# A product over three rows padded to 128 rows in a transform and two-layer mixture kernel on one Trainium2 core

## The chip, the core and the metric

The kernel runs on one NeuronCore of a Trainium2 chip. The metric is the device time of one execution in microseconds. TensorE (PE; its weight loads are listed apart as PEld), VectorE (DVE), ScalarE (ACT), GpSimd (POOL) and SyncE (SP, which issues DMAs) each run their own queue in the order in which the program wrote it.

## The reference

`x` has 8 batches of 3072 tokens of 256 numbers.

```python
X = np.fft.fft(x, axis=1)
X = np.fft.fft(X, axis=2)
x = X.real.reshape(B * S, D)              # 24576 tokens
h = x @ w_in                              # 256 -> 2048
g = np.maximum(h, 0.0) + np.log1p(np.exp(-np.abs(h)))
x = g @ w_out                             # 2048 -> 256
...
logits = xn @ en.T / tau                  # 8 experts, the best one is taken
h = np.maximum(x[mask] @ w1[e], 0.0)
out[mask] = gate_w[mask, None] * (h @ w2[e])
```

## The kernel before

Every product is done in fp16 with operands split in a high and a low part, so a product of two matrices is three: high by high, high by low, low by high.

**Phase 1** holds the transform, the first layer pair and the routing. The transform of a batch has two parts. `fft_a` transforms over a factor of 48 of the token axis (tile `psa`, result `U_s`); its inputs are folded and split in `x_split`, mostly on GpSimd (L487 to L492, L594 to L596). `fft_bc` then makes, for each of 8 tiles of a batch, the transform over the features (`psb`, evacuated to `vh` and `vl`) and the rest of the token axis (`psc`, evacuated to `pqh` and `pql`).

The real part of the transform is symmetric: tokens m and S - m share their cosine part and differ in the sign of the sine part. The kernel therefore keeps an even part P and an odd part Q of a tile (192 columns, 193 in the first tile of a batch), and folds `w_in` likewise. The even part has 129 features (0 to 128) and the odd one 127. A TensorE product contracts at most 128 rows, so feature 128 of the even part stands alone: the product `psd` (L705 to L712) makes its row three times over, by a weight operand that repeats one column three times, and L714 to L718 turn it into the tile `r3` (`pq3`) with the rows (high, high, low). Its partner `w128_s` holds the rows (high, low, high) of the weight row 128, filled by three DMAs (L396). One three-row product then stands for the three split products of that feature.

A **unit** is one tile by a quarter of the 2048 hidden features (four blocks of 128): 8 batches x 8 tiles x 4 quarters = 256 units. For each unit:

- `uv_u`: the even part `pu`, four groups of four products (L745 to L748), the last of each with the three-row operands;
- `uv_v`: the odd part `pv`, four groups of three products (L760 to L762);
- ScalarE copies `pu` to `h` (L772), DVE adds and subtracts `pv` (L779, L780), which gives the two mirrored halves of the tokens;
- softplus: ScalarE's Abs, Exp and Ln (L788, L793, L797), then DVE (L802);
- the split of the result: `gh` on GpSimd (L813 to L817), `gl` on DVE (L826);
- `unit_g2`: the products with `w_out` into three accumulators `G`, and at a tile's end the copies to `rows` (L863) and the router.

The order is written out by hand. Each iteration of the main loop names the steps in a string (`ORDER`): `pu` and `pv` of the present unit, the softplus of the one before, `gl` of the one before that, `G` of the one three back, and between them up to three steps of a transform (`f1`, `f2`, `f3`), the scale of the next batch and the router. The transform of batch b + 1 runs beside the units of batch b, `fft_a` in about the first half of them, `fft_bc` in the second. `pu` and `pv` have one PSUM tile each, and the transform has one bank (`F`) for all its products.

```python
mm(o, win_s[:, 0, 0, fs], hh[:, 0, 0:n], True, False)
mm(o, win_s[:, 0, 0, fs], ll[:, 0, 0:n], False, False)
mm(o, win_s[:, 0, 1, fs], hh[:, 0, 0:n], False, False)
mm(o, w128_s[:, fs], r3[:, 0:n], False, True)
```

All matmuls stand on one line (L205, the helper `mm`), so the profile tells them apart by tile: `pu`, `pv`, `psd`, `G`. In the trace `w128_s` is called `w_s` and `r3` is called `pq`.

**Phase 2** (from about 2430 us) gathers the routed tokens of each expert and runs the expert's two layers (`psH`, `psO`).

Of the kernel before, what the change touches and what calls it, by code (L numbers as in the profile page):

```python
# [79 lines left out]
def _tables():  # L80
    scale = 2.0 ** 13
    qs = [(0, 0), (24, 0)]
    for k1 in range(1, 24):
        qs += [(k1, 0), (k1, 1)]
    fa = np.zeros((96, 2, 48))
    a = np.arange(48)
    for q, (k1, im) in enumerate(qs):
        c, s = _trig(a * k1, 48)
        for bb in range(2):
            fa[2 * a + bb, bb, q] = -s if im else c  # L90
    fa = fa.reshape(96, 96)
    # x[d] + x[256-d], x[d] - x[256-d]; for d = 0 x[0] + x[128], x[0] - x[128]
    c, s = _trig(np.arange(129)[:, None] * np.arange(129)[None], 256)
    db = np.zeros((128, 385))
    db[:, 0:129] = c[0:128]
    db[0, 1:129:2] = 0.0
    db[0, 130:258:2] = 1.0
    db[1:, 258:385] = s[1:128, 1:128]
    pos = np.arange(64)
    bv = 32 * (pos % 2) + pos // 2  # L100
    mc, ms = [], []
    for g, cl in enumerate(_columns()):
        m = np.array(cl)[None]
        c, s = _trig(bv[:, None] * m, S)
        if g == 0:
            z = m % 48 == 0
            mc.append(np.concatenate([c * z, c * ~z]))
            ms.append(np.concatenate([-s * z, -s * ~z]))
        else:
            mc.append(np.concatenate([c, s]))  # L110
            ms.append(np.concatenate([-s, c]))
    mcs = np.stack([np.concatenate(mc, 1), np.concatenate(ms, 1)], 1)
    out = {}
    for n, t in (("fa", fa), ("db", db), ("mcs", mcs)):
        hi = (t * scale).astype(np.float16)
        lo = (t * scale - hi.astype(np.float64)).astype(np.float16)
        out[n] = np.ascontiguousarray(np.stack([hi, lo], 1))
    tid = np.zeros((128, NB * NT * 3), np.int32)
    cols = _columns()
    for b in range(NB):  # L120
        for ti in range(NT):
            cl = sum(cols[3 * ti:3 * ti + 3], [])
            toks = cl + [(S - m) % S for m in cl[2 if ti == 0 else 0:]]
            o = (b * NT + ti) * 3
            tid[:, o:o + 3] = (np.array(toks) + b * S).reshape(3, 128).T
    out["tid"] = tid
    out["ident"] = np.eye(128, dtype=np.float32)
    tri = np.zeros((128, 256), np.float16)
    tri[:, :128] = np.triu(np.ones((128, 128)), 1)
    tri[:, 128:] = 1.0  # L130
    out["tri"] = tri
    misc = np.zeros((128, 128 + 8 + 8 + 8), np.float32)
    misc[:, :128] = np.arange(128)[None]
    misc[:, 128:136] = (E - np.arange(E))[None]
    misc[:, 136:144] = (np.arange(E) * CAP)[None]
    misc[2, 144] = -1.0
    misc[1:, 145] = 1.0
    out["misc"] = misc
    return out
# [3 lines left out]
def fft_moe_moe(ctx, tc, x, w_in, w128, w_out, emb, tau, w1, w2, fa, db, mcs, tid, ident, tri, misc, out,  # L143
# [23 lines left out]
    U_s = bigf.tile([128, 2, 2, 48, 64], F16, name="U_s")       # hi/lo, c, q, pos  # L167
# [7 lines left out]
    win_s = big.tile([128, 2, 2, FF], F16, name="win_s")      # (even, odd) x (hi, lo)  # L175
    w128_s = big.tile([3, FF], F16, name="w128_s")
# [19 lines left out]
    def fps(name):  # L196
        """a bank for the transform and for small products; at the start four of them in turn."""
        if boot[2]:
            boot[1] = (boot[1] + 1) % 4
            if boot[1]:  # L200
                return psG.tile([128, 512], F32, tag=f"G{boot[1] - 1}", name=name)
        return psF.tile([128, 512], F32, tag="F", name=name)
# [4 lines left out]
    # A background chain is a generator: a plain yield lets the others go on; a yield of a pair of  # L207
    # functions asks for a small product (the first) in spare PSUM columns and its readers (the second).
    jobs = []

    class Chain:
# [3 lines left out]
        def step(self):  # L215
            """one step; False when the chain has ended."""
            if self.wait:
                return True
            r = next(self.gen, 0)
            if r == 0:  # L220
                return False
            if r is not None:
                self.wait = True
                jobs.append((self, r))
            return True
# [21 lines left out]
    def bcast_max(col, dst):  # L247
        """dst[128,1] = max over the partitions of col[128,1]."""
# [10 lines left out]
    def expo(dst, src):  # L259
        """dst (f32) = biased exponent of src."""  # L260
        u = sm.tile([128, 1], U32, tag="exu", name="exu")
        V.tensor_single_scalar(u, src.bitcast(U32), 23, op=ALU.logical_shift_right)
        V.tensor_copy(dst, u)

    def pow2(dst, be):
        """dst = 2^(be-127); be is f32."""
# [5 lines left out]
    # just below the words of the smallest magnitude that float32 holds as a normal number  # L272
    THR = float(np.uint32((897 << 20) - 1).view(np.float32))

    def cast(dst, lo, hi, t1, stage, item=None):
        """float64 words to float32 in three stages, in place; 0 for all of them."""
# [18 lines left out]
    class Cast:  # L295
        """pairs (source, target) of float64 words and float32, the low bits cut off, too small ones to zero, in steps;
        mxw gets the largest magnitude of each by the high words, read as float32."""
# [15 lines left out]
        def step(self, stage):  # L313
            """the next item through stage 0 (bits), 1 (mask) or 2 (product)."""
# [38 lines left out]
    def field(i, e11):  # L353
        """e11 = the float64 exponent field of the largest magnitude."""
# [18 lines left out]
    def win_scale():  # L373
        # the row for 128 as 128 x 16
# [24 lines left out]
    def win_fold(k):  # L399
        """W[i] + W[256-i] and W[i] - W[256-i], split; 512 columns."""  # L400
# [14 lines left out]
    def emb_prep():  # L415
        """normalised expert embedding, transposed."""
# [21 lines left out]
    def wout_prep():  # L438
        """w_out with w_out @ en^T as eight more columns, split."""
# [44 lines left out]
    def x_fold(xt, eng):  # L484
        """x[d] + x[256-d] and x[d] - x[256-d] in place."""
# [19 lines left out]
    def fft_scale(b, full=True):  # L505
        """sum of squares of x[b] and the powers of two that follow from it."""
# [92 lines left out]
    def fft_pre(b):  # L599
        """the first two parts of x[b], split."""  # L600
# [13 lines left out]
    def fft_a(b):  # L614
        """U[d, q, pos] of batch b: the transform over a of s = 64 a + pos."""
# [3 lines left out]
        for k in range(8):  # L619
# [3 lines left out]
            for c in range(2):  # L623
                ps = fps("psa")
                for j in range(4):
                    o = ps[:, j * 96:(j + 1) * 96]
                    cs = slice(c * 128, (c + 1) * 128)
                    if boot[0] and PEF:
                        # the fold as a sum of products
# [30 lines left out]
    def fft_bc(b, ti):  # L660
        """P, Q and the row k=128 for tile ti of batch b."""
# [22 lines left out]
        r3 = pqp.tile([3, CN], F16, tag="pq3", name="pq3")  # L684
# [21 lines left out]
        for s in range(3):  # L706
# [3 lines left out]
            o = ps[0:3, off:off + n1]  # L710
            for q, (v, d) in enumerate(((vh, 0), (vh, 1), (vl, 0))):
                mm(o, v[:, s, 128:129].to_broadcast([128, 3]), mcs_s[:, d, 0, coff[g]:coff[g] + n1], q == 0, q == 2)  # L712
        p3 = sm.tile([3, CN], F32, tag="p3", name="p3", bufs=1)
        A.activation(p3[:, 0:n], ps[0:3, 0:n], AF.Copy, scale=2.0 ** -16)  # L714
        h3 = sm.tile([3, CN], F16, tag="h3", name="h3", bufs=1)
        A.activation(h3[:, 0:n], ps[0:3, 0:n], AF.Copy, scale=2.0 ** -16)
        # rows (hi, hi, lo)
        V.scalar_tensor_tensor(r3[:, 0:n], h3[:, 0:n], m3_s[0:3], p3[:, 0:n], op0=ALU.mult, op1=ALU.add)  # L718
# [13 lines left out]
    # one unit: four blocks of 128 hidden features of one tile  # L732
# [122 lines left out]
    def x2_out(b, ti, tt):  # L855
        """x2 and the raw logits of one 128-token block to SBUF, and the squares' sum."""
# [100 lines left out]
    # The first slots need no final numbers: K0 of them go to the expert with the most rows when all pairs but the last  # L957
    # ones are through (an eighth of them at least), K1 to the expert with the most rows that are left then.
# [36 lines left out]
    def snapshot():  # L995
        """the experts of the first slots; their weights and first rows."""
# [6 lines left out]
        for k, n in enumerate((K0, K1)):  # L1003
# [8 lines left out]
            # the expert and its first row that is not done  # L1012
# [20 lines left out]
    def p2_table():  # L1033
        """expert and first row of the other slots: the pairs of tiles of 128 rows, then up to E single tiles (the odd
        ones from the end, the halves of pairs beyond the pair slots from the front: with 2 a + b <= 2 NPS + E - 1
        for a pairs and b odd ones there is room for all)."""
# [19 lines left out]
        # what the first row gains from one expert to the next  # L1056
# [68 lines left out]
    def p2_split(j):  # L1125
        rows = S2[j]["rows"]
        xs = p2["a"].tile([128, 2, 2, 256], F16, tag="xs", name="xs", bufs=1)       # t, hi/lo
# [6 lines left out]
    def p2_tr(j):  # L1134
        xs, nt = S2[j]["xs"], S2[j]["nt"]
        S2[j]["xT"] = xT = p2["a"].tile([128, 2, 2, 2, 128], F16, tag="xT", name="xT")       # t, hi/lo, c
# [111 lines left out]
    def wprep(wpp):  # L1248
        """the experts' weights, scaled and split in two fp16 parts, to DRAM."""
# [59 lines left out]
    with tc.manual_schedule():  # L1309
# [16 lines left out]
        V.memset(half, 0.5)  # L1326
        V.memset(thr_s, -THR)
# [232 lines left out]
```

## Time and profile before

| | before |
|---|---|
| median of 3 runs | 3552.29 us (3549.78 to 3557.27) |
| span of the profiled execution, first to last instruction | 3543.1 us |
| the median less that span | 9.2 us |
| busy share of the span: PE, DVE, ACT, POOL | 92%, 78%, 59%, 59% |
| mean granted TensorE clock | 0.965 |

The profiled execution is known by its span; the runs' times also hold what lies around it. Busy shares are means over stretches with different limits, so the sections below look at stretches apart. TensorE products are pipelined: one that "takes" 0.25 us can start 0.08 us after the one before it, so the distance from start to start is what TensorE spends.

### The profile page before, as it was taken

To read this page: it belongs to the slowest core of one execution; us is meant where nothing else is said; L and a number is where in the kernel's file an instruction comes from. 1 tells how busy PE (TensorE), PEld (TensorE's weight loads), DVE (VectorE), ACT (ScalarE), POOL (GpSimd) and SP (SyncE) were. 2 spreads that over 40 slices of the span, in tenths; PEclk is the share of its full clock that TensorE was granted. 3 is DMA by queue.
4 is the path that set the end of the run, shared out by engine and by line. 5 is a ranking of instruction groups with operands and counts; after the bars stand their busy time and mean duration, and the time that the engine had idled before them with its cause. 6 is when DMAs were issued, how large, how long until landed. Compare 5 with 4: busy or idle time off the path is not lost.

```text
span 3543.1 us, 75429 instructions
## 1 busy us (share of the span) xinstructions
PE 3266.7 (92%) x31264; PEld 2672.1 (75%) x31264; DVE 2750.6 (78%) x3997; ACT 2091.6 (59%) x2904; POOL 2097.1 (59%) x1856
## 2 busy tenths in 40 slices
PE   3888989998998998999899899998889999999998
PEld 3666767766776776676677677777778888888888
DVE  7688898888888898888888888897536665656665
ACT  5766767766876776786687677775223333333332
POOL 5378797689689779878868966775211212122221
PEclk7899999999999999999999999999999999999999
DMA  4202111110210210211121011103673232323321
GB/s 136 77 15 65 42 56 55 43 52 25 64 58 29 71 48 28 74 35 46 41 65 40 31 34 36 41 28 97 150 189 78 76 79 76 79 75 77 77 76 45
DMA packets 197080, 222.03 MB, mean 63 GB/s; under 512 B 119028, under 2 KB 154751, under 8 KB 196480
## 3 DMA queue, kind: packets, MB, share of 16 engines
q1 hardware_dynamic: 177920, 166.46, 17.5%
q0 software_dynamic: 18816, 50.75, 4.2%
q8 instruction: 244, 4.00, 0.5%
q14 instruction: 100, 0.82, 0.1%
HBM read 122.09 MB, written 69.88 MB: 54 GB/s over the span
## 4 chain that ended last, share of the span: by engine, by line
PE 55%; POOL 17%; DVE 17%; issue 4%; ACT 4%; DMA 3%; SPq 0%; POOLq 0%; DVEq 0%; ACTq 0%
PE psO L205 14%; PE psH L205 14%; PE G L205 13%; PE pu L205 7%; PE pv L205 4%; DVE e L802 4%; POOL xl L596 4%; POOL gh L813 3%; DVE gl L826 3%; POOL xh L595 2%; DMA xT<-xs 2%; DVE h L780 2%; POOL xt L594 2%; DVE h L779 2%; PE psb L205 2%
## 5 line engine op out<-in xcount | busy, mean ns | idle before, releaser
L205 PE MATMUL G<-wo_s,gh 128*128 128x264 f16 x6144 | 836.4, 284 | 53.3 <-POOL gh L813 38.8
L813 POOL TENSOR_SCALAR gh<-e,sc 128x1536 f16<-128x1536 f32 (+1 forms) x256 | 552.6, 2159 | 348.7 <-DVE e L802 165.2
L205 PEld LDWEIGHTS <-gh 128*128 128x128 f16 x6144 | 598.0, 100 | 164.1 <-POOL gh L813 41.3
L1186 POOL DMA_INDIRECT out_dram<-ot,r x200 | 196.6, 983 | 840.4 <-ACT ot L1184 806.9
L1160 DVE SCALAR_TENSOR_TENSOR hl<-psH,hh 128x512 f16<-128x512 f32 (+1 forms) x416 | 268.2, 666 | 407.8 <-ACT hh L1159 407.8
L205 PE MATMUL psH<-xT,wb 128*128 128x256 f16 (+1 forms) x4992 | 542.9, 269 | 2.3 <-DVE hl L1160 2.2
L802 DVE SCALAR_TENSOR_TENSOR e<-h,e 128x1536 f32<-128x1536 f32 x256 | 503.3, 1966 | 52.6 <-ACT e L797 52.0
L205 PEld LDWEIGHTS <-win_s 128*128 128x128 f16 x6144 | 463.3, 99 | 102.1 <-issue 5.1
L205 PE MATMUL psO<-wb,hh 128*128 128x256 f16 x3200 | 537.4, 275 | 0.0
L826 DVE SCALAR_TENSOR_TENSOR gl<-e,sc,gh 128x1536 f16<-128x1536 f32 (+1 forms) x256 | 464.9, 1816 | 91.7 <-POOL gh L813 74.4
L205 PEld LDWEIGHTS <-wb 128*128 128x128 f16 x4992 | 473.5, 98 | 55.6 <-issue 2.6
L205 PE MATMUL psO<-wb,hl 128*128 128x256 f16 x1600 | 440.0, 275 | 23.9 <-DVE hl L1160 23.9
L205 PE MATMUL G<-wo_s,gl 128*128 128x264 f16 x3072 | 437.6, 279 | 22.9 <-DVE gl L826 22.9
L788 ACT ACTIVATE e<-h 128x1536 f32<-128x1536 f32 x256 | 377.9, 1476 | 124.4 <-DVE h L780 108.5
L205 PE MATMUL pu<-pqh,win_s 128*128 128x192 f16 (+1 forms) x2048 | 435.4, 253 | 0.0
L1159 ACT ACTIVATE hh<-psH 128x512 f16<-128x512 f32 (+1 forms) x416 | 240.4, 581 | 291.0 <-PE psH L205 291.0
L797 ACT ACTIVATE e<-e 128x1536 f32<-128x1536 f32 x256 | 378.5, 1478 | 3.2
L793 ACT ACTIVATE e<-e 128x1536 f32<-128x1536 f32 x256 | 377.7, 1476 | 0.0
L772 ACT ACTIVATE h<-pu,sc 128x768 f32<-128x768 f32 (+1 forms) x256 | 230.7, 901 | 240.6 <-PE pu L205 204.1
L1184 ACT ACTIVATE ot<-psO,gm 128x256 f32<-128x256 f32 x200 | 94.9, 474 | 462.8 <-PE psO L205 424.8
L205 PEld LDWEIGHTS <-gl 128*128 128x128 f16 x3072 | 302.5, 99 | 79.1 <-DVE gl L826 30.1
L952 POOL DMA_INDIRECT bucket<-rows,dst x192 | 277.1, 1443 | 124.9 <-DVE dst L946 61.8
(272 smaller groups left out, 5867.9 us busy)
## 6 DMA issues: line engine op xcount, KB each, us to landing
xt<-in_x_dram SPq DMA_DIRECT2D x114, 384.0 KB, 4.0
r<-bucket SPq DMA_DIRECT2D x96, 260.0 KB, 2.7
wt<-in_w_dram SPq DMA_DIRECT2D x16, 1024.0 KB, 6.6
wsc<-wo SPq DMA_DIRECT2D x32, 512.0 KB, 3.1
W<-wsc SPq DMA_DIRECT2D x32, 512.0 KB, 5.9
raw<-in_w_in_dram SPq DMA_DIRECT2D x8, 512.0 KB, 7.9
raw<-in_w_out_dram SPq DMA_DIRECT2D x8, 512.0 KB, 3.6
wb<-wsc SPq DMA_DIRECT2D x2, 2048.0 KB, 8.7
```

Source lines behind the costliest of these rows:

```text
L205: T.matmul(o, l, r, start=start, stop=stop)
L772: A.activation(h[:, :, 0:n], d["pu"][:, :, 0:n], AF.Copy, scale=scal[u[0]]["inv"])
L788: A.activation(e, h, AF.Abs)
L793: A.activation(e, e, AF.Exp, scale=-1.0)
L797: A.activation(e, e, AF.Ln, bias=1.0)
L802: V.scalar_tensor_tensor(flat(d["e"]), flat(d["h"]), 0.0, flat(d["e"]), op0=ALU.max, op1=ALU.add)
L813: G.tensor_scalar(gh[:, 0:n], e[:, 0:n], sg, 1.0, op0=ALU.mult, op1=ALU.mult)
L826: V.scalar_tensor_tensor(flat(d["gl"]), flat(d["e"]), scal[u[0]]["sg"], flat(d["gh"]), op0=ALU.mult, op1=ALU.subtract)
L952: no_dep(G.indirect_dma_start(out=bucket, out_offset=bass.IndirectOffsetOnAxis(ap=dst[:, k:k + 1], axis=0), in_=rows[:, k, 0:RW], in_offse ...
L1159: A.activation(h2, p_, AF.Relu)
L1160: V.scalar_tensor_tensor(l2, p_, 0.0, h2, op0=ALU.max, op1=ALU.subtract)
L1186: no_dep(G.indirect_dma_start(out=out, out_offset=bass.IndirectOffsetOnAxis(ap=rows.bitcast(I32)[:, t, 256:257], axis=0), in_=ot, in_offse ...
```

## The change

`w128_s` and `r3` become 128 rows high. `w128_s` is cleared at the start and its first three rows are filled as before, so rows 3 to 127 add nothing. The row for feature 128 is now made 128 times over (the weight operand repeats its column 128 times), and the two copies and the combine work on 128 rows. The arrangement of the steps is the same on every engine; DVE has one instruction more, the memset.

```diff
-    w128_s = big.tile([3, FF], F16, name="w128_s")
+    w128_s = big.tile([128, FF], F16, name="w128_s")
...
-        r3 = pqp.tile([3, CN], F16, tag="pq3", name="pq3")
+        r3 = pqp.tile([128, CN], F16, tag="pq3", name="pq3")
...
-            o = ps[0:3, off:off + n1]
+            o = ps[:, off:off + n1]
             for q, (v, d) in enumerate(((vh, 0), (vh, 1), (vl, 0))):
-                mm(o, v[:, s, 128:129].to_broadcast([128, 3]), mcs_s[:, d, 0, coff[g]:coff[g] + n1], q == 0, q == 2)
-        p3 = sm.tile([3, CN], F32, tag="p3", name="p3", bufs=1)
-        A.activation(p3[:, 0:n], ps[0:3, 0:n], AF.Copy, scale=2.0 ** -16)
-        h3 = sm.tile([3, CN], F16, tag="h3", name="h3", bufs=1)
-        A.activation(h3[:, 0:n], ps[0:3, 0:n], AF.Copy, scale=2.0 ** -16)
+                mm(o, v[:, s, 128:129].to_broadcast([128, 128]), mcs_s[:, d, 0, coff[g]:coff[g] + n1], q == 0, q == 2)
+        p3 = sm.tile([128, CN], F32, tag="p3", name="p3", bufs=1)
+        A.activation(p3[:, 0:n], ps[:, 0:n], AF.Copy, scale=2.0 ** -16)
+        h3 = sm.tile([128, CN], F16, tag="h3", name="h3", bufs=1)
+        A.activation(h3[:, 0:n], ps[:, 0:n], AF.Copy, scale=2.0 ** -16)
...
-        V.scalar_tensor_tensor(r3[:, 0:n], h3[:, 0:n], m3_s[0:3], p3[:, 0:n], op0=ALU.mult, op1=ALU.add)
+        V.scalar_tensor_tensor(r3[:, 0:n], h3[:, 0:n], m3_s, p3[:, 0:n], op0=ALU.mult, op1=ALU.add)
...
         V.memset(half, 0.5)
+        V.memset(w128_s.bitcast(U32), 0)
         V.memset(thr_s, -THR)
```

## Rows read from the trace of the kernel before

**Rows 1.** The page's first part: busy us of each engine, share, instructions.
```profile
PE 3266.7 (92%) x31264; PEld 2672.1 (75%) x31264; DVE 2750.6 (78%) x3997; ACT 2091.6 (59%) x2904; POOL 2097.1 (59%) x1856
```

**Rows 2.** Table by stretch: from:to, length, each engine's busy us, clock, DMA.
```profile
95.70:442.50 346.80, 299.89 (x2932) 234.44 (x2931) 285.51 (x394) 243.82 (x348) 239.51 (x186) 0.93 0.16 47
442.50:2194.70 1752.20, 1622.91 (x15842) 1264.01 (x15840) 1534.99 (x2037) 1271.12 (x1641) 1399.02 (x1061) 0.96 0.15 47
1612.20:1767.80 155.60, 134.49 (x1251) 102.98 (x1249) 133.51 (x157) 99.91 (x119) 140.62 (x103) 0.95 0.10 32
1767.80:1904.20 136.40, 134.80 (x1398) 106.89 (x1396) 120.70 (x189) 113.22 (x159) 94.92 (x77) 1.00 0.22 67
2194.70:2430.00 235.30, 232.18 (x2079) 181.46 (x2078) 209.27 (x296) 181.87 (x198) 162.46 (x129) 1.00 0.14 49
```

**Rows 3.** The page's groups: count | busy, mean ns | idle before, releaser.
```profile
L772 ACT ACTIVATE h<-pu,sc 128x768 f32<-128x768 f32 (+1 forms) x256 | 230.7, 901 | 240.6 <-PE pu L205 204.1
```

**Rows 4.** Timeline of PE in one unit: start us, us, product, shape, count.
```profile
1500.88 0.24 PE L205 MATMUL pu<-pqh,win_s 128*128 128x192 f16 x1
...
1501.04 0.25 PE L205 MATMUL pu<-pqh,win_s 128*128 128x192 f16 x1
1501.22 0.25 PE L205 MATMUL pu<-pq,w_s 3*128 3x192 f16 x1
1501.40 0.26 PE L205 MATMUL pu<-pqh,win_s 128*128 128x192 f16 x1
...
1503.01 0.26 PE L205 MATMUL pv<-pqh,win_s 128*128 128x192 f16 x1
...
1504.02 1.06 PE L205 MATMUL G<-wo_s,gh 128*128 128x264 f16 x8
```

**Rows 5.** Groups of weight loads by shape, columns as in rows 3.
```profile
L205 PEld LDWEIGHTS <-win_s 128*128 128x128 f16 x6144 | 463.3, 99 | 102.1 <-issue 5.1 <-DVE h L780 1.1
L205 PEld LDWEIGHTS <-w_s 3*128 3x128 f16 x1024 | 92.7, 90 | 165.0 <-issue 164.9 <-DMA raw<-in_w_out_dram 0.2
```

**Rows 6.** The same timeline of PE: `psc`, and `psd` between two `G`.
```profile
1500.34 0.23 PE L205 MATMUL psc<-mcs_s,vh 128*128 128x64 f16 x2
...
1505.02 0.22 PE L205 MATMUL psd<-mcs_s,vh 128*3 128x64 f16 x2
...
1505.38 0.85 PE L205 MATMUL G<-wo_s,gh 128*128 128x264 f16 x6
```

**Rows 7.** Groups of ScalarE by shape.
```profile
L678 ACT ACTIVATE vh<-psb 128x256 f16<-128x256 f32 x64 | 24.3, 380 | 21.0 <-PE psb L205 20.8
L714 ACT ACTIVATE p<-psd 3x192 f32<-3x192 f32 x56 | 17.4, 311 | 9.8 <-PE psd L205 8.5
```

**Rows 8.** Timeline of DVE at the start; in brackets idle time and what ended it.
```profile
0.84 0.17 DVE L1325 MEMSET ones<- 128x128 f32 x1 [0.84 <-PEq L1550]
...
3.67 0.17 DVE L1328 COPY base_s<-misc_s 128x8 f32<-128x8 f32 x1 [2.64 <-DMA misc_s<-in_misc_dram]
```

**Rows 9.** Waits of DVE, 1767.8 to 1904.2: us in total, times, longest.
```profile
DVE e L802 <- ACT e L797: 5.3, 10, 1.0
DVE h L779 <- ACT h L772: 4.3, 4, 1.7
DVE h L779 <- PE pv L205: 4.0, 5, 1.6
```

**Rows 10.** Longest waits of DVE and PE, 1612.2 to 1767.8.
```profile
DVE gl L826 <- POOL gh L813: 14.5, 4, 5.5
...
PE G L205 <- POOL gh L813: 7.1, 2, 4.2
PE psa L205 <- DVE U_s L644: 6.8, 4, 2.6
```

**Rows 11.** Timeline of PE: the first products after a stall.
```profile
1635.86 1.50 PE L205 MATMUL G<-wo_s,gh 128*128 128x264 f16 x6 [4.21 <-POOL gh L813]
```

**Rows 12.** Table by stretch, columns as in rows 2.
```profile
1634.80:1641.40 6.60, 4.89 (x22) 3.04 (x23) 5.52 (x6) 0.10 (x1) 6.04 (x8) 0.50 0.27 82
```

## The prediction

> **What bounds the kernel now.** I read the page first, then a table of five stretches, then the order of TensorE's instructions within one unit, then the waits. The engines' line [rows 1] makes TensorE (PE) the busiest engine, 92% of the span, with VectorE (DVE) next at 78%; an average like that says too little, so the table follows [rows 2]. Its columns are the length of the stretch and each engine's busy time. The first stretch is the start and batch 0, the second batches 1 to 6, the fifth batch 7, which has no transform beside it. The third and fourth split one batch (5) into its two halves: in the third the transform over `a` of the next batch (its splits are GpSimd work) runs beside the units, in the fourth the rest of that transform.
>
> In the fourth stretch PE is busy 134.8 of 136.4 us and in the fifth 232.2 of 235.3: PE sets the pace there. In the third PE is idle 155.6 - 134.5 = 21.1 us, and GpSimd (POOL) is busy 140.6 of 155.6 (90%): there POOL and DVE set the pace. The second stretch holds six such batches: PE idle 129.3, DVE idle 217.2.
>
> Now the place of the change [rows 4]. These are the starts of PE's products. In the odd part (`pv`, all 128-row operands) twelve products take 1503.01 to 1504.02, 84 ns each. In the even part (`pu`) a group of four starts at 1500.88, its third product at 1501.04, the three-row product at 1501.22 and the next group at 1501.40: two steps of 0.08, then 0.18 into the three-row product and 0.18 out of it. The product itself is no longer than its neighbours (0.25 against 0.24); the time lies in the steps. The weight loads say it too [rows 5]: ahead of the 1024 three-row loads PE's load path sat idle 165.0 us, 161 ns each, released by nothing ("issue"), though each load takes 90 ns, like the others.
>
> **The change part by part.**
> *Three-row product made 128 rows.* If the fourth product steps like those of `pv`, the sixteen products of a unit take 16 x 0.084 = 1.34 us instead of 1501.40 - 1500.88 = 0.52 to 0.54 a group, 2.13 for the unit (1500.88 to 1503.01): 0.79 us less. There are 256 units [rows 3]: 202 us of PE time. Below, this could be nothing (the step stays 0.18); above, no row is shorter than 0.08.
>
> *The operand's own product (`psd`) made 128 columns wide.* Now PE goes from `G` to the three-column product and back [rows 6]. Eight `G` products from 1504.02 at about 0.113 would let the next start at 1504.93; it starts at 1505.02. At 30 ns each, the step of `psc` below, its nine products end their turn at 1505.29, when `G` could follow; it comes at 1505.38: 0.09 on each side, 0.18 us. One per tile, 64 tiles: 12 us of PE time. Within the nine I take no change: 128-column products of the same width, `psc`, step at 30 ns too (18 from 1500.34 to the next at 1500.88). Their weights are read contiguously and these are one column repeated, which no row shows at 128; if each of the 576 stepped like `G`, the widest load-bound step here, 576 x 0.083 = 48 us of PE time come back. I take the nearest row, `psc`.
>
> So PE's work falls by 214 us, nearly all of it inside the units.
>
> *ScalarE and DVE on 128 rows instead of 3.* Two copies (L714, L716) and one combine (L718) per tile, same length along the free axis. ScalarE's copy of 128 x 256 out of PSUM takes 380 ns, the three-row copy of 192 takes 311 [rows 7]: at most 69 ns x 128 = 9 us, and nearer to nothing as the first is a third longer along the free axis; ScalarE idles 23 us in each second half alone. Nothing for DVE on the same grounds: the free size is what these rows follow.
>
> *One memset of 128 x 1024 words on DVE at the start.* The row for 128 x 128 is 0.17 us [rows 8]; eight times that is 1.4 us, and behind it DVE waits 2.64 us for its first load. Hidden; without that cover 1.4 us. The three DMAs that fill rows 0 to 2 come long after it in DVE's order. Instruction order is otherwise the same on every engine.
>
> **What of 214 us reaches the end.** Where PE is late, its neighbours idle; they say how much they can take.
> - Second halves (the fourth stretch, 16 units): PE's work falls by 16 x 0.79 + 1 = 14 to about 121 us. DVE has 136.4 - 120.7 = 15.7 idle, of which 13.6 are three waits for ScalarE or PE [rows 9]; ScalarE's own idle time is mostly a wait for `pu` [rows 3], which comes 0.8 us earlier. DVE then becomes the engine that is never free, at about 123 us. At most 13 us are to be had; I take 9, as the queues will not fit without gaps.
> - First halves (the third stretch): DVE's longest wait is for POOL's `gh`, 14.5 us, and PE's two longest are for `gh` and the transform's DVE copy [rows 10]. POOL is idle 15 us in all, part of it its own DMA issue. PE will reach the same POOL bursts earlier and wait longer. I take 4.
> - Six batches: 6 x 13 = 78. A second way to it: over the second stretch DVE is busy 1535 us, against PE's new 1623 - 192 x 0.79 - 48 x 0.18 = 1463, so DVE becomes the tightest engine; the old length was 1752 / 1623 = 1.08 times the tightest, and 1.08 x 1535 = 1658 is 94 less than now. I keep the smaller figure, since DVE's busy time leaves out its short gaps.
> - Batch 7: PE's work falls by 32 x 0.79 = 25; DVE is idle 26. I take 15.
> - The start and batch 0: PE idle 46.9, DVE 61.3, both waiting on the set-up. I take 8.
>
> Sum 78 + 15 + 8 = 101 us. Phase 2, from 2430 on, has none of these products and only starts earlier. The span 3543.1 becomes 3442; the runs' median lies 9.2 above this span (6.7 to 14.2), so **3451 us**.
>
> The weight loads themselves last alike, 90 ns of three rows and 99 ns of 128 [rows 5]; only the steps between products differ, 0.18 against 0.08, and the sum goes by the steps. A rule that speaks against the change: the Trainium skill, "TensorE: Matmul & The Clock Gate", section "LDWEIGHTS (loading the stationary operand)", says that a load of 32 rows takes as long as one of 128, since only columns count; by it alone the term of 202 would be nothing and the time 3552. The durations agree with it, the steps say that it is not the whole cost.
>
> **The rivals.**
> 1. *The gain goes through almost whole.* If DVE and POOL can be packed, batches 1 to 6 give up to 13 + 9 each, batch 7 22, the start 15: 150 to 190, centre 170, 3382. For it: in the second halves all of DVE's waits lead back to PE. Against: POOL at 90% in the first halves.
> 2. *A new wait takes its place.* The transform has a single PSUM bank, so its second product of a unit must wait for ScalarE and DVE to empty the first; `pu` stands between and gets 0.8 us shorter, so PE may arrive early and wait there. If second halves give 4, first halves 1, batch 7 8 and the start 2, the gain is 40: 3512. For it: 6.8 us of `psa` waiting on DVE already [rows 10]. Against: hardly any such wait in the second halves.
> 3. *No change.* The 0.18 steps belong to the place (last of a group, an operand of another tile), not to the row count: 3552. Against: the first product of the next group, a plain one, steps 0.18 too, and the `psd` edges show the same at three columns. (The skill's rule on weight loads, above, would come out here.)
> 4. *Slower.* PE's new idle time lets its granted clock fall to the lower level (1.2 instead of 2.4 GHz). After a stall of 4.21 us [rows 11] it stood at 0.50 from 1634.8 to 1641.4, and 22 products ran in these 6.6 us [rows 12], where `pv`'s step gives 79; at half the clock such a stretch costs about 3.3 us of PE work. The second halves now stand at 1.00. It decides from 101 / 3.3 = 31 further stretches that nothing absorbs, five in each of the six batches; at eight in each, 48 x 3.3 = 158 us come back and the time is 3609. Against: the waits I expect are under 1 us, and the fall shown came with one of 4 us.
>
> **How the numbers follow.** Forecast (gain 60 to 145) 0.70; rival 1, 0.10; rival 2 (gain 10 to 60) 0.14; rival 3, 0.03; rival 4, 0.03. The range reaches from a gain of 155 (into rival 1) to one of 45 (into the better half of rival 2): 3397 to 3507; it leaves out most of rival 1, the poorer half of rival 2, and 3 and 4, some 0.2. A difference of 0.2%, 7 us, is about what a measurement of this kernel can tell. Faster by more than that: the forecast, rival 1 and nearly all of rival 2, 0.94; within it 0.03; slower 0.03.
>
> **What would show each step.** In the order of products `pu` should step at 0.083 throughout, and the load path's 165 us of idle ahead of these loads should be gone; the `G`-`psd` edges should lose 0.09 each. In the table PE's busy share of the second halves should fall below 95% and DVE's rise to 94 to 97%, the waits "h from pu" of ScalarE shrink most, and the first halves should keep their length within 6 us. The prediction is wrong if the steps stay at 0.18 (rival 3), if PE's new idle time stands at `psb` or `psc` (rival 2), if the clock in the second halves drops below 1.00 (rival 4), or if the first halves shorten as much as the second (rival 1).

## The result and the profile after

| | before | changed |
|---|---|---|
| median of 4 runs each, on one chip | 3551.68 us (3549.78 to 3557.27) | 3511.69 us (3510.47 to 3513.20) |
| ratio of the runs, 95% interval | | 0.9892 (0.9876 to 0.9908) |
| span of the profiled execution | 3543.1 us | 3510.3 us |
| mean granted clock | 0.965 | 0.957 |

Faster by 40 us in the medians, where 101 were forecast; 3512 lies 5 us outside the range.

TensorE's steps shrank as they were to. The timeline of PE in one unit of the changed kernel (columns as in [rows 4]):

```profile
1479.13 0.25 PE L205 MATMUL pu<-pqh,win_s 128*128 128x192 f16 x1
...
1479.30 0.25 PE L205 MATMUL pu<-pqh,win_s 128*128 128x192 f16 x1
1479.38 0.25 PE L205 MATMUL pu<-pq,w_s 128*128 128x192 f16 x1
1479.46 0.25 PE L205 MATMUL pu<-pqh,win_s 128*128 128x192 f16 x1
...
1480.45 0.25 PE L205 MATMUL pv<-pqh,win_s 128*128 128x192 f16 x1
```

The steps into and out of the padded product are 0.08, and the sixteen products take 1.32 us instead of 2.13 [rows 4]. The padded loads have lost the idle time ahead of them, 165.0 us in [rows 5]:

```profile
L205 PEld LDWEIGHTS <-w_s 128*128 128x128 f16 x1024 | 102.0, 100 | 0.5
```

The edges of `psd` are gone as well; the same timeline around it, against [rows 6]:

```profile
1473.91 1.06 PE L205 MATMUL G<-wo_s,gh 128*128 128x264 f16 x8
1474.81 0.23 PE L205 MATMUL psd<-mcs_s,vh 128*128 128x65 f16 x2
...
1475.09 1.06 PE L205 MATMUL G<-wo_s,gh 128*128 128x264 f16 x8
```

Eight `G` at 0.113 end their turn at 1474.81, nine `psd` at 0.03 at 1475.08: nothing is lost on either side, and the repeated column loads as fast as any.

The span is 33 us shorter. The table of the same five stretches of the program (columns as in [rows 2], each beginning with the same unit) shows where the rest stayed:

```profile
95.60:440.00 344.40, 274.20 (x2935) 243.95 (x2932) 289.34 (x392) 242.97 (x347) 233.01 (x184) 0.92 0.17 48
440.00:2159.90 1719.90, 1480.55 (x15844) 1310.09 (x15842) 1548.77 (x2040) 1267.77 (x1639) 1397.70 (x1063) 0.95 0.16 48
1593.80:1750.00 156.20, 125.59 (x1250) 107.96 (x1248) 137.48 (x160) 100.34 (x122) 141.16 (x104) 0.92 0.10 32
1750.00:1879.50 129.50, 120.46 (x1397) 110.11 (x1395) 119.42 (x186) 112.08 (x156) 93.27 (x76) 1.00 0.24 70
2159.90:2395.20 235.30, 215.24 (x2090) 189.70 (x2088) 216.02 (x299) 183.57 (x202) 164.30 (x133) 0.97 0.15 51
```

The last row of [rows 2] ends earlier in the program than the last one here: at 2430.0 the kernel before is in a step that the changed one reaches at 2393.0. Up to the same step the kernel before has:

```profile
2194.70:2432.20 237.50, 233.67 (x2090) 182.61 (x2089) 211.40 (x299) 184.07 (x201) 164.49 (x132) 1.00 0.14 50
```

So batch 7 is 2.2 us shorter (237.5 to 235.3), with PE idle 20.1 us instead of 3.8 and DVE busy 216.0 instead of 211.4. Against [rows 2], the first half of batch 5 is 0.6 longer, its second half 6.9 shorter. Added up over batches 1 to 6, the second halves went from 819.5 to 789.9 us and the first halves from 932.7 to 930.0. In every stretch PE's busy time fell, and its idle time rose by half of that or more. From the start to the end of batch 7 the busy time fell by 187 us, where 214 were forecast: in batch 5's second half by 14.3, as forecast, but in batch 7 by 18.4 instead of 25. The granted clock there fell from 1.00 to 0.97, and it fell in three second halves as well, which all stood at 1.00 before, those of batches 1, 2 and 3:

```profile
591.30:731.70 140.40, 125.71 (x1378) 112.78 (x1375) 119.68 (x184) 110.97 (x154) 92.24 (x77) 0.95 0.20 58
887.80:1022.90 135.10, 125.69 (x1398) 113.26 (x1396) 120.84 (x187) 112.39 (x156) 91.48 (x76) 0.96 0.24 70
1178.30:1309.50 131.20, 123.70 (x1397) 111.70 (x1394) 121.10 (x189) 112.21 (x156) 94.54 (x77) 0.97 0.23 69
```

What PE now waits for, over batches 1 to 6 (us in total, times, longest); first the changed kernel:

```profile
PE G L205 <- DVE gl L826: 53.3, 32, 2.7
PE G L205 <- POOL gh L813: 50.8, 16, 5.1
PE psb L205 <- DVE vl L679: 40.3, 23, 3.9
PE psa L205 <- DVE U_s L644: 38.4, 20, 2.8
PE pv L205 <- DVE wpm L1264: 21.0, 8, 7.2
```

and the same five in the kernel before:

```profile
PE G L205 <- POOL gh L813: 37.7, 10, 4.2
PE psa L205 <- DVE U_s L644: 27.9, 17, 2.6
PE G L205 <- DVE gl L826: 21.3, 17, 1.9
PE pv L205 <- DVE wpm L1264: 16.4, 8, 6.4
...
PE psb L205 <- DVE vl L679: 7.7, 8, 1.4
```

204 us instead of 111, spread over five places, four of which wait for DVE and one for GpSimd. ScalarE's wait for `pu`, 204.1 us in [rows 3], is the one that shrank, as it should; over the 224 copies of this shape it went from 174.1 to 56.7 us:

```profile
L772 ACT ACTIVATE h<-pu,sc 128x768 f32<-128x768 f32 x224 | 201.8, 901 | 111.6 <-PE pu L205 56.7 <-DVE rs L894 23.2 <-DVE e L802 22.2
```

**Theory 1**: DVE is the next limit, so what PE gets back turns into PE waiting for DVE. **Theory 2**: GpSimd's bursts hold it. Rival 2 of the prediction (one PSUM bank for the transform) had named the very time, 3512; whether its reason is the right one needed a test too, as the wait that it names, `psb` for DVE, grew from 7.7 to 40.3 us.

### The profile page after: what moved, and what is told of

It is laid out like the page before. It is cut to its first block, busy times and chain, and to the rows that moved or that the text cites. A ratio compares the mean times of both kernels' runs of the same rounds, so it can differ in the third digit from the quotient of the medians.

```text
span 3510.3 us, 75430 instructions
## 1 busy us (share of the span) xinstructions
PE 3085.3 (88%) x31264; PEld 2736.4 (78%) x31264; DVE 2773.5 (79%) x3998; ACT 2086.2 (59%) x2904; POOL 2088.7 (60%) x1856
## 4 chain that ended last, share of the span: by engine, by line
PE 39%; DVE 25%; POOL 17%; ACT 8%; issue 6%; DMA 4%; another core or an unknown queue 0%; SPq 0%; POOLq 0%; DVEq 0%; ACTq 0%
PE psO L205 14%; PE psH L205 13%; PE G L205 6%; DVE e L802 6%; DVE gl L826 4%; POOL xl L596 4%; POOL gh L813 3%; DVE h L780 2%; DVE h L779 2%; DMA xT<-xs 2%; POOL xh L595 2%; ACT e L797 2%; PE pu L205 2%; POOL xt L594 2%; ACT e L793 2%
## 5 line engine op out<-in xcount | busy, mean ns | idle before, releaser
L205 PE MATMUL G<-wo_s,gh 128*128 128x264 f16 x6144 | 850.8, 287 | 77.8 <-POOL gh L813 56.1
L802 DVE SCALAR_TENSOR_TENSOR e<-h,e 128x1536 f32<-128x1536 f32 x256 | 513.7, 2007 | 42.2 <-ACT e L797 35.5
L826 DVE SCALAR_TENSOR_TENSOR gl<-e,sc,gh 128x1536 f16<-128x1536 f32 (+1 forms) x256 | 473.9, 1851 | 87.3 <-POOL gh L813 69.9
L205 PEld LDWEIGHTS <-win_s 128*128 128x128 f16 x6144 | 530.5, 99 | 6.9 <-DVE h L780 3.5
L205 PE MATMUL G<-wo_s,gl 128*128 128x264 f16 x3072 | 448.6, 284 | 62.7 <-DVE gl L826 61.8
L205 PE MATMUL pu<-pqh,win_s 128*128 128x192 f16 (+1 forms) x2048 | 370.8, 251 | 0.0
L205 PEld LDWEIGHTS <-hh 128*128 128x128 f16 x3200 | 315.4, 99 | 42.9 <-issue 2.4
```

Of the source, the lines that this page charges most:

```text
L205: T.matmul(o, l, r, start=start, stop=stop)
L802: V.scalar_tensor_tensor(flat(d["e"]), flat(d["h"]), 0.0, flat(d["e"]), op0=ALU.max, op1=ALU.add)
L826: V.scalar_tensor_tensor(flat(d["gl"]), flat(d["e"]), scal[u[0]]["sg"], flat(d["gh"]), op0=ALU.mult, op1=ALU.subtract)
```

## The experiments

### What the extra steps hang on: 64 and 96 rows

```diff
-    w128_s = big.tile([128, FF], F16, name="w128_s")
+    w128_s = big.tile([64, FF], F16, name="w128_s")
...
-        r3 = pqp.tile([128, CN], F16, tag="pq3", name="pq3")
+        r3 = pqp.tile([64, CN], F16, tag="pq3", name="pq3")
```

and likewise for `psd`, `p3`, `h3` and the combine; in the second kernel 96.

> The changed kernel padded to 64 rows instead of 128. If the extra step comes with any operand that uses half of the array's rows or fewer, the steps in and out stay at 0.18 us and the time is that of the kernel before, 3545 to 3560. If it comes only with very few rows, the steps are 0.08 and the time is that of the changed kernel, 3505 to 3520.

> Padded to 96 rows. The transform's products over 96 rows follow plain ones without an extra step in the trace of before, so the steps should be 0.08 and the time that of the changed kernel, 3505 to 3520. If only all 128 rows avoid the step, it stays at 0.18 and the time is 3545 to 3560.

Measured: 64 rows 3545.38 us, 1.0002 of the kernel before (0.9991 to 1.0014); 96 rows 3503.96, 0.9885 (0.9858 to 0.9912), a ratio no different from that of 128 rows (on this chip the kernel before takes 3544.83 us). The timeline of PE, first with 64 rows and then with 96:

```profile
1502.77 0.25 PE L205 MATMUL pu<-pqh,win_s 128*128 128x192 f16 x1
1502.95 0.25 PE L205 MATMUL pu<-pq,w_s 64*128 64x192 f16 x1
1503.14 0.26 PE L205 MATMUL pu<-pqh,win_s 128*128 128x192 f16 x1
```

```profile
1506.27 0.25 PE L205 MATMUL pu<-pqh,win_s 128*128 128x192 f16 x1
1506.35 0.25 PE L205 MATMUL pu<-pq,w_s 96*128 96x192 f16 x1
1506.44 0.25 PE L205 MATMUL pu<-pqh,win_s 128*128 128x192 f16 x1
```

Steps of 0.18 and 0.19 at 64 rows, 0.08 and 0.09 at 96. The number of rows alone does it, somewhere between 64 and 96: the step costs 0.10 us more on each side. The Trainium skill, "TensorEngine Tiling (Array Packing)", section "Tiling Modes", says that the array can be used as tiles of 32, 64 or 128 rows and that changing the mode, as against the tile, drains TensorE. These rows fit that, with the 0.10 us as the price of a change; they show the step, and not the mode.

### The operand's own product alone

```diff
-            o = ps[0:3, off:off + n1]
+            o = ps[:, off:off + n1]
...
-                mm(o, v[:, s, 128:129].to_broadcast([128, 3]), ...)
+                mm(o, v[:, s, 128:129].to_broadcast([128, 128]), ...)
```

> The kernel before with one part of the change alone: the operand's own product is made 128 columns wide, the three-row product of the units stays. If the sum's step holds, the nine products step at 30 ns and the two edges lose 0.09 us each: 12 us less PE work, of which 2 to 8 us reach the end; 3541 to 3549 against 3549. If a repeated column at 128 loads slowly, PE's work grows by up to 48 us and the time by 10 to 45.

Measured: 3539.44 us against 3544.83, ratio 0.998 (0.9967 to 0.9992), 5 us of the 12 that PE gains, within the first bounds. Too few columns of an operand cost a step on each side as too few rows do.

### Is it DVE? Half of one DVE step left out, in both kernels

```diff
-        V.scalar_tensor_tensor(flat(d["e"]), flat(d["h"]), 0.0, flat(d["e"]), op0=ALU.max, op1=ALU.add)
+        V.scalar_tensor_tensor(flat(d["e"])[:, 0:768], flat(d["h"])[:, 0:768], 0.0, flat(d["e"])[:, 0:768], op0=ALU.max, op1=ALU.add)
```

> The kernel before, with the DVE step that adds the maximum to the softplus (L802) done on half its columns only; the other half keeps the logarithm alone. It takes about 1.0 us of DVE from each of 256 units, 250 us in all, and nothing from PE. Theory 1 (DVE is the next limit once PE is freed): TensorE still sets the pace here, so little is gained, 3552 falls to 3470 to 3515. Theory 2 (GpSimd, not DVE, holds what PE gave): the same small gain.

> The changed kernel with the same half of L802 left out. Theory 1: the padded operand now gives 120 to 170 us instead of 40, so 3512 falls to 3320 to 3390, and the last batch, which gained nothing, shortens by 15 to 25 us more than in the same cut of the kernel before. Theory 2: the difference to the same cut of the kernel before stays below 70 us.

Measured: 3446.41 (ratio 0.9724, 0.970 to 0.9748) without the padding and 3364.72 (0.9477, 0.9461 to 0.9492) with it. Without the padding more was gained than either theory expected, 103 us, 72 of them in the first halves (932.7 to 860.1 us over the six). With it the padding is worth 82 us instead of 40: above the 70 of theory 2 and short of the 120 of theory 1. Tables by stretch, batches 1 to 6 and batch 7; first without the padding, then with it:

```profile
425.80:2097.40 1671.60, 1602.58 (x15843) 1258.40 (x15840) 1377.04 (x2037) 1268.76 (x1641) 1323.03 (x1060) 0.98 0.16 49
2097.40:2330.80 233.40, 232.91 (x2090) 182.84 (x2088) 181.29 (x298) 182.80 (x200) 157.85 (x132) 1.00 0.15 51
```

```profile
420.90:2038.60 1617.70, 1454.56 (x15843) 1297.83 (x15840) 1386.64 (x2038) 1263.44 (x1639) 1324.72 (x1061) 0.97 0.16 51
2038.60:2254.50 215.90, 208.53 (x2090) 189.08 (x2088) 187.15 (x299) 182.48 (x203) 156.79 (x132) 0.99 0.16 55
```

Batch 7, which gained 2.2, now gains 17.5 us of the 25 that PE was to save there. Batches 1 to 6 gain 53.9 instead of 32.3, all but 0.3 of it in the second halves: 811.5 to 757.9 us over the six, 53.6 instead of 29.6. In these two kinds of stretch it was DVE's work that held most of the gain. The first halves of batch 5 are 144.6 and 144.3 us: nothing, still.

### Is it GpSimd? Part of its split left out, in both kernels

```diff
-            x_fold(xt, V if k in (FW1 if b == 1 else FW) else G)
+            if k in (FW1 if b == 1 else FW):
+                x_fold(xt, V)
...
-            G.tensor_scalar(xt, xt, sx, 1.0, op0=ALU.mult, op1=ALU.mult)
+            if boot[0]:
+                G.tensor_scalar(xt, xt, sx, 1.0, op0=ALU.mult, op1=ALU.mult)
```

> The kernel before, with GpSimd's part of the split of x after the start made lighter: its three folds of a batch (4.3 us each) and its scaling of each eighth (1.4 us) left out, about 24 us a batch, all in the first halves. Theory 2 (GpSimd's bursts bound the first halves): 3552 falls by 40 to 100. Theory 1: by less than 60, as DVE and PE stay as they are.

> The changed kernel with the same GpSimd work left out. Theory 2: the padded operand gives 90 us or more against the same cut of the kernel before, the first halves of the batches shorten by 8 us or more each. Theory 1: the difference stays between 40 and 70 us, the first halves gain no more than 3 us each.

Measured: 3421.06 (ratio 0.9635, 0.9619 to 0.9651) and 3383.90 (0.9522, 0.9494 to 0.955). Both kernels gain about 128 us, more than either theory had put down for the first, and the padding stays worth 37: far from the 90 of theory 2 and just under the 40 to 70 of theory 1. The first half of batch 5 without the padding, then with it:

```profile
1525.90:1662.70 136.80, 128.66 (x1251) 101.03 (x1249) 131.79 (x157) 99.82 (x119) 115.94 (x86) 0.99 0.11 36
```

```profile
1504.00:1638.90 134.90, 117.76 (x1250) 104.06 (x1249) 133.44 (x159) 100.33 (x122) 114.46 (x86) 0.97 0.12 37
```

Both are 19 to 21 us shorter than with GpSimd's full work, and still the padding brings only 2: with GpSimd lighter, DVE is the one with little idle time (5.0 us left, then 1.5). So theory 2 is right that GpSimd's work sets the length of the first halves (DVE's does too: its cut took 11 us off the same half), and wrong as a reason why the padding gave so little: take GpSimd's work away and DVE stands behind it.

### Is it the transform's one PSUM bank?

```diff
-ORDER = "sp ab f1 pu s1 eu ex pv ev q1 G0 f2 ln p1 G1 q2 ...
+ORDER = "sp ab f1 pu s1 eu ex pv ev q1 G0 ln p1 G1 f2 q2 ...
```

> The changed kernel with the second transform step of an iteration moved behind the second group of G products, so that ScalarE and DVE have some 1.6 us more to empty the one PSUM bank. If the wait for that bank (psb for the DVE copy vl, 40 us over batches 1 to 6, 8 before) is what took the gain, 15 to 40 us come back: 3472 to 3497. If DVE's own load is what took it, PE waits elsewhere instead and the time moves by less than 10 us.

Measured: 3513.94 us, ratio 0.9907 (0.9876 to 0.9937), the changed kernel's own. PE's waits over batches 1 to 6:

```profile
PE G L205 <- DVE gl L826: 63.2, 45, 2.8
PE G L205 <- POOL gh L813: 48.9, 15, 5.0
...
PE psc L205 <- DVE vl L679: 14.9, 21, 1.8
...
PE psb L205 <- DVE vl L679: 3.6, 3, 1.4
```

The wait of `psb` for `vl` fell from 40.3 to 3.6 us and other waits took its place. The time as a whole did not move, but it moved between the halves: added up over batches 1 to 6 the second halves went from 789.9 to 781.0 us and the first halves from 930.0 to 938.6. Batch 1's second half, 140.4 us at a clock of 0.95 in the changed kernel, is now:

```profile
590.50:723.90 133.40, 120.88 (x1377) 108.93 (x1374) 119.01 (x182) 111.76 (x152) 92.15 (x76) 1.00 0.19 60
```

Seven of the 9 us stand in this one half, and some 2 us of GpSimd's work in a batch moved from the second halves to the first with the step. So the wait at the bank can be a part of what batch 1 lost; for the kernel as a whole, taking nearly all of that wait away gave nothing. Rival 2 had the right time, and its reason is at most a small part of the cause.

### Spending PE's free time: the fold on TensorE, and GpSimd's split moved

The start of the kernel folds x by three more products for each output instead of on DVE and GpSimd. The first edit does so in all batches, in both kernels; `fan`, the negated table, moves to a pool that lives long enough.

```diff
-        if not boot[0]:
-            x_fold(xt, V if k in (FW1 if b == 1 else FW) else G)
...
-                    if boot[0] and PEF:
+                    if PEF:
```

> The kernel before, with the fold of x left to TensorE in all batches (as the start does it already): three more products of 96 columns for each output, 192 a batch at 0.042 us, 8 us more PE work in the first halves, where PE idles 20; DVE loses five folds of 2.2 us a batch and GpSimd three of 4.3 us. Both theories expect a gain: 3545 falls to 3470 to 3525.

> The changed kernel with the fold left to TensorE. If DVE and GpSimd hold what PE was given, spending freed PE time to unload them pays: the first halves shorten by 8 to 14 us each, the time falls to 3415 to 3465, and the padded operand is worth 50 to 90 us against the same fold in the kernel before. If the first halves are bound by the order of the steps and not by these two engines' work, less than 3 us each come back, 3490 to 3515.

Measured: 3470.74 (ratio 0.9781, 0.9759 to 0.9802) and 3419.62 (0.9639, 0.9623 to 0.9655): both as expected, the padding worth 51. The fold on TensorE brings 78 us without the padding, where the first halves left PE idle already, and some 90 with it: most of what it brings does not hang on the padding.

The second edit names splits that go to ScalarE and DVE: `FA = FA1 = (1, 4, 5)`, without the fold on TensorE.

> The changed kernel with three of the eight splits of a batch moved from GpSimd (6 us each) to ScalarE (1.05) and DVE (2.1). If GpSimd's bursts alone bound the first halves, they shorten by 8 us or more each: 3440 to 3465. If DVE is as near its limit there, the 6 us that DVE gains eat it: 3495 to 3520.

Measured: 3580.37 us, ratio 1.0092 (1.0075 to 1.0109): slower than both kernels, and both expectations missed. The waits of ScalarE, DVE and PE over batches 1 to 6, the largest of each:

```profile
ACT xh L591 <- POOL xt L492: 168.7, 17, 14.7
```

```profile
DVE xl L592 <- ACT xh L591: 123.4, 17, 9.2
```

```profile
PE psa L205 <- DVE U_s L644: 113.1, 30, 10.6
```

These three splits are the ones whose fold stays on GpSimd (in batch 1 two of them). ScalarE's copy now stands at the head of its queue until GpSimd has folded, DVE's step behind it until ScalarE has copied, and everything queued behind these two, the units' own work included, stands with them.

With the fold on TensorE that wait has nothing to wait for. The last kernel has both: the fold as above, and `FA = FA1 = (1, 5)`.

> The fold left to TensorE and two splits of a batch moved to ScalarE and DVE. DVE has then 11 us less and 4 more, GpSimd 25 less. If both engines bound the first halves together, this beats the fold alone by 10 to 40 us; if DVE alone does, it is 5 to 25 us slower than the fold alone.

Measured: 3386.51 us (3378.55 to 3394.82), ratio 0.9551 (0.9532 to 0.9570): 33 us better than the fold alone, within the bounds for two engines that hold the first halves together, and 162 us better than the kernel before, with the whole computation in it. It was not run without the padding. Batch 5's two halves:

```profile
1495.50:1634.50 139.00, 123.80 (x1443) 111.82 (x1441) 130.94 (x152) 102.64 (x124) 119.83 (x88) 0.99 0.12 37
1634.50:1765.70 131.20, 123.71 (x1397) 111.73 (x1395) 118.42 (x185) 111.71 (x156) 94.78 (x78) 0.97 0.22 68
```

The first half is 17 us shorter than in the changed kernel (156.2) although it holds more of PE's work, 1443 products against 1250; PE still idles 15 us of it.

The padding's worth in four settings, from the medians above: 40 us as it was changed, 37 with less GpSimd work, 51 with the fold on TensorE, 82 with less DVE work. In batches 1 to 6 of the profiled executions alone it is 32.3, 32.2, 36.5 and 53.9 us, so only the lighter DVE changes it much. With the fold on TensorE a further 15 us stand before batch 1, which begins at 440.1 us without the padding and at 424.9 with it; but that point differs by some 8 us between two padded kernels with the same steps up to there (440.0 with 128 rows, 432.3 with 96).

## Why the prediction was wrong

**The steps on TensorE held.** 202 us for the units: the steps are 0.08 and the unit's sixteen products 1.32 us, 0.81 less than before where 0.79 was taken. 12 us for `psd`: 0.18 per tile, confirmed, and alone worth 5 us of time. No slow loads of a repeated column. At the full clock the sum holds for a stretch too (14.3 us in batch 5's second half, where 14 was taken); other stretches, several of them at a lower clock, gave less, and of 214 us 187 came. ScalarE's copies on 128 rows take 330 and 332 ns against 311 and 303 (2.9 us in all), the memset 0.91 us where 1.4 was the bound, hidden as said.

**What failed is the step "What of 214 us reaches the end".** It took the neighbours' idle time as time that could be had, most of all DVE's. The runs showed in its place that DVE's work holds most of the gain: with half of one DVE step left out, the same padding gives 53.6 us in the second halves and 17.5 in batch 7, about the 54 and 15 that were put down, and as the kernel stood it gave 29.6 and 2.2. The first halves gave next to nothing in every setting.

| term | forecast, us | measured, us |
|---|---|---|
| second halves, batches 1 to 6 | 54 | 29.6 |
| first halves, batches 1 to 6 | 24 | 2.7 |
| batch 7 | 15 | 2.2 |
| start and batch 0 | 8 | 2.4 |
| what lies behind batch 7 | 0 | -4.2 |

- "Batch 7: DVE is idle 26. I take 15": 2.2. DVE's idle time there fell by 7 us only, of which 4.6 went into longer DVE steps (busy 211.4 to 216.0) and 2.2 into a shorter batch. PE's waits there in the changed kernel:

```profile
PE G L205 <- DVE gl L826: 7.3, 11, 1.4
PE pv L205 <- DVE wpm L1264: 5.6, 2, 3.2
PE G L205 <- POOL gh L813: 5.3, 1, 5.3
```

  Some 19 us of waits that came to 3 before. With DVE lighter by a half step the same batch gives 17.5. Here an engine 89% busy, whose steps come in a fixed order between those of others, did not have its 11% to give.
- "First halves: I take 4" each: 0.5. Neither with less DVE work nor with less GpSimd work, nor with less of both and the fold on TensorE (144.6 and 143.8 us), was the padding worth more than 2 us in the first half of batch 5. Less GpSimd work or less DVE work shortens it by 11 to 21 us, less PE work does not. No run takes work from both without adding to PE, so which order of steps holds it then stays open.
- "Second halves: 9 of 13": 4.9 on average, 6.9 in batch 5, 10.2 in batch 6 (134.2 to 124.0), and 2.8 lost in batch 1 (137.6 to 140.4). DVE did not become the engine that is never free: in batch 5 it stands at 119.4 of 129.5 us, 92%, below the 94 to 97% that I had put down, and PE with 120.5 is still the busier.
- "The start and batch 0": 2.4 of 8. Both engines were said to wait on the set-up; DVE's largest wait in that stretch was for `pv` (14.6 us). As the point where batch 1 begins differs by some 8 us between two padded kernels (above), one execution of each can't tell 2.4 from 8. The 4.2 us that were lost behind batch 7, where nothing was changed, are likewise not explained.
- The check by "1.08 times the tightest engine" was no check: the factor is 1719.9 / 1548.8 = 1.11 now, with two engines close in load (PE 1480.6, DVE 1548.8).
- The basis was off by 7 us. Executions of which both are known take 1.9 us more than their span (3512.17 and 3510.3 here), so the profiled one of before took some 3545, less than the runs' median; I had taken the 9.2 between as lying around the span. In spans the gain is 32.8.

**Rival 4 came in part,** by its own sign: the clock of the second halves dropped below 1.00 in three of six (0.95, 0.96, 0.97), and in batch 7 from 1.00 to 0.97, as PE's stalls grew. The first halves, at 0.91 to 0.95 before, stand at 0.92 to 0.93. At 0.03 of 235 us it is 7 us of PE time in batch 7; as PE waits there anyway, what it cost the end was not tried. For the second halves some runs tell: that of batch 5 takes 129.5 us at 1.00 in the changed kernel, and 131.2 at 0.97 in the last kernel above and in the padded one with less GpSimd work:

```profile
1638.90:1770.10 131.20, 123.71 (x1398) 111.82 (x1395) 120.88 (x187) 112.14 (x156) 94.56 (x77) 0.97 0.23 69
```

At 1.7 us for 0.03, the three dips come to some 7 of the 24 us that the second halves lack, an estimate. **Rival 1** needed DVE and GpSimd to be packable, and they were not. **Rival 2** named 3512 and a single bank; the wait at the bank did grow, but with the step moved it is nearly gone and the time stays: the number was met by luck. **Rival 3** is out: at 64 rows the place in the group is the same as at 96, and the steps are not.

## What to carry to other kernels

An operand of few rows or columns between full ones costs TensorE time on each side (here 0.10 us) that no product's duration shows: read start-to-start distances and the idle time ahead of weight loads, and pad above 64 rows. Before you forecast what a freed engine brings, ask which engine is next and halve a piece of its work in both kernels: the difference tells whether the gain is held there. Work taken off the next engines and put on the one with idle time can pay more than freeing that one further: here the padding brought 40 us, the fold on TensorE 78 without the padding and some 90 with it, and the moved split 33 more. Move a step only together with what it waits for, or it blocks its new queue.

## What was not expected of the hardware

- The step appears at 64 rows with the same 0.18 and 0.19 us as at 3, and is gone at 96; columns (3 against 128) cost 0.09 us per side likewise.
- With 96 columns `psd` has no such edge either, but its nine products take 0.38 us, where they take 0.27 with 3 or with 128 columns. The timeline of PE with 96 rows:

```profile
1500.76 1.07 PE L205 MATMUL G<-wo_s,gh 128*128 128x264 f16 x8
1501.67 0.24 PE L205 MATMUL psd<-mcs_s,vh 128*96 128x64 f16 x2
...
1502.05 1.07 PE L205 MATMUL G<-wo_s,gh 128*128 128x264 f16 x8
```

- One DVE step (L802) lasted longer in the changed kernel, 2007 ns on average against 1966, with the same operands and as many times; first the changed kernel's group, then the one of before. The median is 1758 ns in both, so some executions grew, not all (53 of 256 last over 2000 ns, 43 before); what they ran into was not tried.

```profile
L802 DVE SCALAR_TENSOR_TENSOR e<-h,e 128x1536 f32<-128x1536 f32 x256 | 513.7, 2007 | 42.2 <-ACT e L797 35.5 <-issue 5.9
```

```profile
L802 DVE SCALAR_TENSOR_TENSOR e<-h,e 128x1536 f32<-128x1536 f32 x256 | 503.3, 1966 | 52.6 <-ACT e L797 52.0
```
